# Recurrent-scan attention with a gated unit: order of the result buffers, of the last loads and of the w_o splits

## The chip, the cores and the metric

The kernel runs on one core of a Trainium2 chip. A core has a matrix engine (TensorE, PE in the profile), VectorE (DVE), ScalarE (ACT) and GpSimd (POOL), and a queue engine, SyncE (SP), from which all transfers of this kernel are issued. Each engine works through its own instructions in order and waits at its head for what it needs. The metric is the device time of one execution in microseconds (us); lower is better. Three executions of the kernel before took 2379.27, 2383.05 and 2387.33 us; the median is 2383.05 us.

## The reference

With x of 2048 rows (tokens) and 1024 columns, all float32:

```python
xn = layernorm(x)
q, k, v = split(xn @ wqkv)                     # 32 heads of 32 columns
pq, pk = q @ w_phi, k @ w_phi                  # per head
phi_q = [softmax(pq), softmax(-pq)]            # 64 features a head
phi_k = [softmax(pk), softmax(-pk)]
kv, z = phi_k^T v, sum over tokens of phi_k    # no causal mask
o = (phi_q kv) / (phi_q z + 1e-6)
s = o @ wo                                     # 1024 x 1024
g = silu(((sigmoid(xn @ w_gate)) * (xn @ w_up)) @ w_down)    # inner width 3584
return x + s * g
```

## The kernel before

**Products.** Each float32 operand of a large product is split in two parts, high and low (`split`, line 174): ScalarE rounds it to the high part (line 176), VectorE subtracts to get the low part (line 177). Three matmuls (`mm3`, lines 181 to 183) then stand for one exact product. The products go by a Strassen-like scheme of seven block products instead of eight. Its seven products are called B11, T2, T3, B21, T1, T4 and B22 (line 92); the operands of the T and B22 ones are sums and differences of blocks. A block that shares terms adds onto the bank of an earlier product: B21 onto B11's bank, T4 onto T3's, B22 onto T1's. Before it does, the earlier product must have been read out of the bank.

**Stages.** (1) x is normalised and transposed. (2) For each half of the tokens, V, K and Q are projected, and the gated unit's inner product follows, some 28 units to a half. (3) `w_down` is multiplied in 98 steps (`dsteps`; the list of B22 is gone through once for each half, 14 steps each), and the gate g is written to memory (`g_d`). (4) The last stage works on eight pairs of row tiles (`for tp_ in range(NTP)`). For each pair it computes `o @ wo` in seven products of 12 matmuls, multiplies with the gate, adds x and stores. Between its matmuls it prepares the next pair (`attend`: transposes of the query features, numerators, sums and splits of o).

**w_o.** Its seven operands are made once, during the second half's projections, in four tasks (`o_task`, line 305). A task loads four blocks and splits B11 and B21, splits T4, lets GpSimd make four sums in a row (T1's, T3's, T2's, B22's), and splits these. `keep` splits into one of three buffers (`o_r`) and stores to `wo_d`. `background` lets a task go a step further behind an evacuation (`proj_out`, line 471). During stages 3 and 4 the operands are loaded again (`wo_prep`, line 767) into buffers that have come free: T3's four into block `x1`, which is new at step `ND - 2 * NJ`, and B21's into former buffers of h.

**w_down's loads.** `down_prep` (line 684) loads a weight block into one of two raw buffers (`wdraw`, line 690) and a piece of h into one of three (lines 696 and 700), then splits both. It runs ahead as far as free buffers allow. Side work (`side`) is taken one item for each step after `ND - 2 * NJ`.

**The last stage's buffers.** `res` holds four half buffers, dealt in the same order to every pair: `u1`, `u2`, `y11`, `y21`. `u1` takes B11 (ScalarE's copy, line 1225), then T2 is added (line 1227), and `u2` is `u1` plus T3 (line 1229). The results are: B21 into `y11` (line 1236), T1 into `u2`, T4 into `y21`, B22 into `u1` (line 1239). Each is multiplied with the gate and added to x, on GpSimd in pieces of 256 columns, or on VectorE for T4 and B22 of the last pair (`eng`, line 1233), and stored (line 1242). `gx_load` (lines 1203 and 1204) fetches the gate and x for a result into a ring of four half buffers, two results deep; the next load is asked for when a result has been stored.

**Order.** The program's text gives priorities. A planner (line 1271) lays the instructions of each engine out by its own estimate of durations, so an instruction can stand earlier or later on its engine than its place in the text: in the last pair T1's product stands before B21's. `tc.issue_after(i)` makes instructions follow instruction `i` on that engine.

Of the kernel before, what the change touches and what calls it, by code (L numbers as in the profile page):

```python
# [91 lines left out]
B11, T2, T3, B21, T1, T4, B22 = range(7)  # L92
# [3 lines left out]
def hedgehog_glu_kernel(  # L96
# [12 lines left out]
    nc = tc.nc  # L109
    pool, vector = Pieces(nc.gpsimd, 256), Pieces(nc.vector, 1024)  # L110
# [21 lines left out]
    h_d = dram.tile([7, NJ, P, NCH, HB], F32, name="h_d")  # L132
    wd_d = dram.tile([7, NJ, P, HB], F32, name="wd_d")
# [26 lines left out]
    def whole(i):  # L160
        return slots[i].rearrange("p a n -> p (a n)")

    def halves(*ids):
        return [slots[i][:, a] for i in ids for a in range(2)]
# [24 lines left out]
    side, last_sp = deque(), []  # L189
# [115 lines left out]
    def o_task(k):  # L305

        def keep(i, b):
            o = slots[o_r.next()]
            split((o[:, 0].bitcast(F32R), o[:, 1].bitcast(F32R)), b)
            nc.sync.dma_start(wo_d[i, k], o.bitcast(F32).rearrange("p a n -> p (a n)"))  # L310

        a11, a12, a21, a22 = bs = halves(47, 52)
        for b, (f, h) in zip(bs, ((0, 0), (0, 1), (1, 0), (1, 1))):
            nc.sync.dma_start(b, wo[(k + 4 * h) * P:(k + 4 * h + 1) * P, f * HB:(f + 1) * HB])
        yield
        keep(B11, a11)
        keep(B21, a12)
        yield
        keep(T4, a22)
        pool.add(a22, a21, a22)  # L320
        pool.sub(a21, a11, a21)
        pool.sub(a11, a22, a11)
        pool.sub(a12, a12, a11)
        yield
        yield
        keep(T2, a11)
        keep(T3, a21)
        yield
        keep(T1, a22)
        keep(B22, a12)  # L330

    o_r = Ring((36, 37, 38))
# [316 lines left out]
    wdraw = Ring(halves(42))  # L649
    yr = Ring(halves(48, 49))  # L650
    sig_r = Ring(halves(53))
    last_split = []

    def wd_block(i, j):
        f, col = {B11: (j, 0), B21: (j + NJ, 0), B22: (j + NJ, 1)}.get(i, (j, 1))
        return w_down[f * P:(f + 1) * P, col * HB:(col + 1) * HB]
# [27 lines left out]
    def down_prep():  # L684
        n = len(dready)
        if n == len(dsteps) or not wfree or len(hfree) < len(dsteps[n][2]):
            return False
        i, j, cs = dsteps[n]
        r = wdraw.next()
        nc.sync.dma_start(r, wd_block(i, j) if i in (B11, B21, B22) else wd_d[i, j])  # L690
        w = wfree.popleft()
        split(pair(w), r)
        r = hraw.next()
        hs = {}
        if len(cs) == 2:
            nc.sync.dma_start(whole(r), h_d[i, j].rearrange("p c n -> p (c n)"))
        for c in cs:
            rc = slots[r][:, c]
            if len(cs) == 1:
                nc.sync.dma_start(rc, h_d[i, j, :, c])  # L700
            hs[c] = hfree.popleft()
            last_split[:] = [split(pair(hs[c]), rc).ins]
        dready.append((w, hs))
        return True
# [49 lines left out]
    NTP = TT // 2  # L754
# [2 lines left out]
          T1: [], T4: [], B22: list(range(4))}  # L757
    phu = Ring((44, 20))
    ofr = Ring((46, 24, 25, 26, 27, 22, 23, 39, 40, 41, 42))
    res = Ring(halves(49, 52))  # L760
    gx = Ring(halves(54, 53))
    tpr, nmr, amm = Ring(banks[:2]), Ring(banks[2:4]), Ring(banks[4:])
    e_next, units_ph, of = [0, 0], {}, {}
    oraw = [slots[50], slots[51]]
# [1 line left out]
    def wo_prep(i, k):  # L766
        nc.sync.dma_start(slots[WO[i][k]].bitcast(F32).rearrange("p a n -> p (a n)"), wo_d[i, k])

    def e_load(u):
        tp_, hb = divmod(e_next[u], 2)  # L770
        if tp_ < NTP:
            nc.sync.dma_start(whole(47 + u), f_d[2 * tp_ + u, hb].rearrange("q s n c -> (q s) (n c)"))
        e_next[u] += 1
# [202 lines left out]
    for n, (kind, c, what, i) in enumerate(ops):  # L976
# [37 lines left out]
        j, s = what  # L1014
# [21 lines left out]
        if i == B11:  # L1036
            u1, u2 = ur.next(), ur.next()
# [5 lines left out]
        else:  # L1043
# [3 lines left out]
            g = gates[q]  # L1047
# [46 lines left out]
    u1, u2 = halves(0, 1, 2, 3), halves(4, 5, 6, 7)  # L1094
# [12 lines left out]
    def evacuate(i, p):  # L1107
# [18 lines left out]
        else:  # L1126
            nc.vector.tensor_add(u1[p], u1[p], b)
            gate_out(u1[p], t, 1)

    ND = len(dsteps)  # L1130
    LQ = 64
    late = [Steps(*[(5, lambda t=t, hb=hb: q_task(t, hb)) for hb in range(2) for t in range(a, TT, 2)]) for a in range(2)]
    for n, (i, j, cs) in enumerate(dsteps):
        w, hs = dready[n]
        for c in cs:
            for u in range(4):
                p = 4 * c + u
                mm3(banks[p], cut(pair(hs[c]), slice(u * P, (u + 1) * P)), pair(w),
                    j == 0 and i in (B11, T2, T3, T1), j == NJ - 1, skip_group_check=True)
        wfree.append(w)  # L1140
        hfree.extend(hs.values())
        if n >= ND - 2 * NJ - 8 and len(WO[B21]) < 4 and hfree:
            WO[B21].append(hfree.popleft())
        if n == LQ:
            assert not last_q.left
            block("fb", 43, 4, F32R)
            for q, s in enumerate(KVB):
                nc.sync.dma_start(slots[s].bitcast(F32), kvbd_d[q])
        while down_prep():
            pass  # L1150
        if j == NJ - 1:
            for c in cs:
                for u in range(4):
                    evacuate(i, 4 * c + u)
        if n == 0:
            assert not any(a.left for a in (early_k, proj1, *beside0, *beside1)) and not kv_due
        if n < 2 * NJ * 3 - 2:
            for a in range(2):
                if late[a].left and (n or not a) and late[a].left > 5 * 16 * (80 - n) // 82 - 3 * a:
                    with tc.issue_after(last_split[0]):  # L1160
                        late[a].step()
        if last_q.left and last_q.left > last_q.total * (LQ - n) // (LQ):
            with tc.issue_after(last_split[0]):
                last_q.step()
        if 40 <= n < 56 and n % 2 == 0:
            wo_prep(*divmod((n - 40) // 2, 4))
        if n == ND - 2 * NJ:
            assert not any(a.left for a in late) and len(WO[B21]) == 4
            block("x1", 4, 4, F32R)
            for i in (T3, B21):  # L1170
                side.extend([lambda i=i, k=k: wo_prep(i, k) for k in range(4)])
            side.extend([lambda u=u: e_load(u) for u in range(2)])
        if n == ND - NJ:
            step(1000)
            side.extend([lambda fn=fn, a=a: fn(*a) for fn, *a in attend(0)])
        if len(dready) == ND:
            for i, free in ((T1, hfree), (T4, wfree)):
                while free and len(WO[i]) < 4:
                    WO[i].append(free.popleft())
                    side.append(lambda i=i, k=len(WO[i]) - 1: wo_prep(i, k))  # L1180
        if n > ND - 2 * NJ:
            step(1 + (n > ND - NJ and n % 2))
# [9 lines left out]
    gxs = {}  # L1192
# [5 lines left out]
    def gx_load():  # L1198
        if result:
            tp_, i = result.pop(0)  # L1200
            t, cols = rows(tp_, i)
            g, xt = gxs[tp_, i] = gx.next(), gx.next()
            nc.sync.dma_start(g, g_d[t, :, cols])
            nc.sync.dma_start(xt, x[t * P:(t + 1) * P, cols])

# [3 lines left out]
    for tp_ in range(NTP):  # L1209
        nxt = attend(tp_ + 1) if tp_ + 1 < NTP else []  # L1210
        n = 0
        u1, u2, y11, y21 = [res.next() for _ in range(4)]
        for i in range(7):
            if i in opening:
                abank[i] = amm.next()
            ps = abank[{B21: B11, T4: T3, B22: T1}.get(i, i)]
            o = [h.rearrange("p (k t) -> p k t", t=P) for h in pair(of[tp_][i])]
            for k in range(4):
                mm3(ps, (o[0][:, k], o[1][:, k]), pair(WO[i][k]), i in opening and k == 0, k == 3, skip_group_check=True)
                n += 1  # L1220
                while nxt and (13 - len(nxt)) * 3 <= 2 * n:
                    fn, *a = nxt.pop(0)
                    fn(*a)
            if i == B11:
                nc.scalar.copy(u1, ps)
            elif i == T2:
                nc.vector.tensor_add(u1, u1, ps)
            elif i == T3:
                nc.vector.tensor_add(u2, u1, ps)
            else:  # L1230
                g, xt = gxs.pop((tp_, i))
                t, cols = rows(tp_, i)
                eng = vector if tp_ == NTP - 1 and i in (T4, B22) else pool
                if i == B21:
                    y = y11
                    nc.vector.tensor_mul(y, g, ps)
                else:
                    y = {T1: u2, T4: y21, B22: u1}[i]
                    nc.vector.tensor_add(y, u2 if i == T1 else u1, ps)
                    eng.mul(y, y, g)  # L1240
                eng.add(y, y, xt)
                nc.sync.dma_start(out[t * P:(t + 1) * P, cols], y)
                gx_load()
# [31 lines left out]
```

## Time and profile before

| what | us |
|---|---|
| median of three executions | 2383.05 |
| lowest and highest | 2379.27, 2387.33 |
| the profiled execution's own time | 2388.2 |
| its span, first to last instruction | 2386.4 |
| TensorE busy in the span | 2350.8 |
| TensorE's longest waits after the start | 3.0 (at 2366.8), 2.8 (at 970.7), 2.4 (at 2115.9) |
| last matmul's end | 2379.95 |

The span starts with the first instruction and ends with the last; the profiled execution's own time is 1.8 us longer. In a row of the timeline stand start, duration, engine, line and operation, and in brackets how long the engine had been idle and what released it. "x4" means four instructions merged into one row. A row of waits gives the sum in us, the number and the longest. In rows of DMA issues "to landing" is the time from the issue until the data are in place.

### The profile page before, as it was taken

The page shows a single profiled execution, that of the slowest core. Times are in us where ns is not written, and L with a number is a line of the kernel's source. Part 1 is how long each engine was busy: PE and PEld are TensorE (multiplying, and loading weights), DVE is VectorE, ACT ScalarE, POOL GpSimd, SP SyncE. Part 2 cuts the span into 40 slices and gives each one's busy share as a digit, 9 for nine tenths or more (in the row PEclk, how much of TensorE's full clock was granted, in tenths as well). Part 3 has the DMA queues.
Part 4 walks back from the last instruction along what each step waited for, and adds up shares of the span by engine and source line. Part 5 has one row for each costly group of instructions (what it writes and reads, how often), then busy time and mean ns, then how long its engine had stood idle before and what let it go on. Part 6 is the DMA issues. An engine that isn't in the chain of part 4 may idle for free. (4 is left out here: it accounts for less than half of the span.)

```text
span 2386.4 us, 32555 instructions
## 1 busy us (share of the span) xinstructions
PE 2350.8 (99%) x10772; PEld 1954.1 (82%) x10772; DVE 1654.7 (69%) x2362; ACT 990.4 (42%) x1478; POOL 1180.2 (49%) x1354
## 2 busy tenths in 40 slices
PE   8999999999999999999999999999999999999998
PEld 6788888878888788788888888888888888878886
DVE  7534778677777675466767878765676776567775
ACT  6433344445454453233444334443443333355442
POOL 4510166777777542304463645454444455434665
PEclk9999999999999999999999999999999999999999
DMA  8874566888888789858887888879777777878654
GB/s 293 281 258 172 176 230 216 271 309 296 298 298 295 278 288 332 316 190 294 264 288 280 278 265 263 282 265 354 249 244 247 260 249 240 285 254 284 210 194 151
DMA packets 266426, 626.24 MB, mean 262 GB/s; under 512 B 37904, under 2 KB 66576, under 8 KB 261648
## 3 DMA queue, kind: packets, MB, share of 16 engines
q1 hardware_dynamic: 266256, 624.15, 77.1%
q8 instruction: 85, 1.39, 0.2%
q14 instruction: 85, 0.70, 0.1%
HBM read 374.47 MB, written 249.56 MB: 261 GB/s over the span
## 5 line engine op out<-in xcount | busy, mean ns | idle before, releaser
L182 PE MATMUL bank<-x,w 128*128 128x512 f32 x2352 | 916.7, 390 | 0.0
L181 PE MATMUL bank<-x,w 128*128 128x512 f32 x2352 | 905.1, 390 | 6.7 <-DVE fb L1052 2.4
L183 PE MATMUL bank<-x,w 128*128 128x512 f32 x2352 | 906.2, 390 | 0.0
L79 POOL TENSOR_TENSOR fc<-fc 128x256 f32<-128x256 f32 x486 | 417.5, 889 | 473.1 <-DMA fc<-e_d 114.0
L177 DVE TENSOR_TENSOR w<-fa,w 128x512 fp32r<-128x512 f32 (+1 forms) x444 | 405.1, 915 | 190.4 <-ACT w L176 185.1
L176 ACT CAST w<-fa 128x512 fp32r<-128x512 f32 (+1 forms) x444 | 307.6, 698 | 539.8 <-PE bank L182 339.1
L181 PEld LDWEIGHTS bank<-x,w 128*128 128x128 f32 x2352 | 442.1, 188 | 101.0 <-DVE fb L1052 3.5
L183 PEld LDWEIGHTS bank<-x,w 128*128 128x128 f32 x2352 | 442.0, 188 | 91.7
L182 PEld LDWEIGHTS bank<-x,w 128*128 128x128 f32 x2352 | 442.2, 188 | 90.1
L181 PE MATMUL bank<-w,x 128*128 128x512 f32 x704 | 276.8, 393 | 5.8 <-DVE fb L471 2.8
L182 PE MATMUL bank<-w,x 128*128 128x512 f32 x704 | 275.6, 391 | 1.8 <-DVE w L177 1.8
L183 PE MATMUL bank<-w,x 128*128 128x512 f32 x704 | 275.8, 392 | 0.9 <-DVE x L177 0.9
L79 POOL TENSOR_TENSOR fb<-fa 128x256 f32<-128x256 f32 x112 | 100.5, 918 | 244.5 <-DMA fa<-w_gu 143.8
L79 POOL TENSOR_TENSOR fb<-fb,fc 128x256 f32<-128x256 f32 x132 | 122.5, 948 | 120.5 <-DVE fc L1059 120.2
L181 PEld LDWEIGHTS bank<-w,x 128*128 128x128 f32 x704 | 132.6, 188 | 34.9 <-issue 3.2
L182 PEld LDWEIGHTS bank<-w,x 128*128 128x128 f32 x704 | 132.7, 189 | 29.3 <-DVE w L177 2.6
L183 PEld LDWEIGHTS bank<-w,x 128*128 128x128 f32 x704 | 132.6, 188 | 28.6 <-DVE x L177 1.8
L79 POOL TENSOR_TENSOR fc<-fc,sa 128x256 f32<-128x256 f32 x128 | 97.2, 790 | 94.3 <-issue 85.1
L176 ACT CAST p<-fc 128x512 fp32r<-128x512 f32 x100 | 75.1, 758 | 160.3 <-DVE fc L537 68.2
L177 DVE TENSOR_TENSOR p<-fc,p 128x512 fp32r<-128x512 f32 x100 | 101.3, 1018 | 53.5 <-ACT p L176 53.2
L177 DVE TENSOR_TENSOR x<-fa,x 128x512 fp32r<-128x512 f32 x112 | 91.4, 817 | 45.2 <-ACT x L176 45.1
L176 ACT CAST w<-fb 128x512 fp32r<-128x512 f32 (+1 forms) x114 | 71.2, 626 | 115.2 <-PE bank L182 88.6
(210 smaller groups left out, 2919.3 us busy)
## 6 DMA issues: line engine op xcount, KB each, us to landing
ws_d<-w SPq DMA_DIRECT2D x112, 512.0 KB, 4.1
w<-ws_d SPq DMA_DIRECT2D x112, 512.0 KB, 5.2
fa<-w_gu SPq DMA_DIRECT2D x84, 512.0 KB, 4.6
fa<-h_d SPq DMA_DIRECT2D x84, 512.0 KB, 5.0
fa<-wf_d SPq DMA_DIRECT2D x32, 1024.0 KB, 6.4
h_d<-fc SPq DMA_DIRECT2D x120, 256.0 KB, 4.5
fa<-w_down SPq DMA_DIRECT2D x80, 256.0 KB, 5.2
h_d<-fb SPq DMA_DIRECT2D x76, 256.0 KB, 4.7
```

Source lines behind the costliest of these rows:

```text
L79: last = self.engine.tensor_tensor(o[:, s], a[:, s], b[:, s], op=op)
L176: nc.scalar.copy(o[0], src)
L177: return nc.vector.tensor_sub(o[1], src, o[0].bitcast(F32))
L181: nc.tensor.matmul(o, a[0], b[0], start=first, stop=False, **kw)
L182: nc.tensor.matmul(o, a[0], b[1], start=False, stop=False, **kw)
L183: nc.tensor.matmul(o, a[1], b[0], start=False, stop=last, **kw)
```

## The change

Five edits:

- `o_task` splits T1 and T3 first, then T2 and B22, in two steps as before. Before, T2 and T3 came first, then T1 and B22.
- `last_load` remembers the last load issued by `down_prep`. The loads of w_o for T3 come after those for B21 and the two `e_load` in the side work, and each is put behind the last load so far (`behind_load`).
- `res` is a plain list, and after each pair it is re-dealt: the next pair's `u1` is this pair's `y11`, `u2` stays, `y11` becomes `y21`, and `y21` becomes `u1`.
- Gate and x of the last pair go into eight half buffers of their own (`last_gx`, slots 47, 48, 50 and 51: those of the query features and of the raw operands), and whatever of them is still to be loaded when the last pair starts is loaded at once.
- In the last pair GpSimd multiplies the gates of T4 and B22 with `u1` as soon as T2 is in it and adds the product to x. Afterwards VectorE multiplies T4's and B22's banks with the gate and adds that sum: two passes over 512 columns where there were three.

```diff
@@ o_task @@
+        keep(T1, a22)
+        keep(T3, a21)
+        yield
         keep(T2, a11)
-        keep(T3, a21)
-        yield
-        keep(T1, a22)
         keep(B22, a12)
@@ down_prep @@
-        nc.sync.dma_start(r, wd_block(i, j) if i in (B11, B21, B22) else wd_d[i, j])
+        last_load[:] = [nc.sync.dma_start(r, wd_block(i, j) if i in (B11, B21, B22) else wd_d[i, j]).ins]
...
@@ last stage's buffers @@
-    res = Ring(halves(49, 52))
-    gx = Ring(halves(54, 53))
+    res = halves(49, 52)
+    gx, last_gx = Ring(halves(54, 53)), Ring(halves(47, 48, 50, 51))
...
+    def behind_load(f, *a):
+        with tc.issue_after(last_load[0]):
+            f(*a)
...
             block("x1", 4, 4, F32R)
-            for i in (T3, B21):
-                side.extend([lambda i=i, k=k: wo_prep(i, k) for k in range(4)])
+            side.extend([lambda k=k: wo_prep(B21, k) for k in range(4)])
             side.extend([lambda u=u: e_load(u) for u in range(2)])
+            side.extend([lambda k=k: behind_load(wo_prep, T3, k) for k in range(4)])
...
-            g, xt = gxs[tp_, i] = gx.next(), gx.next()
+            ring = last_gx if tp_ == NTP - 1 else gx
+            g, xt = gxs[tp_, i] = ring.next(), ring.next()
...
-        u1, u2, y11, y21 = [res.next() for _ in range(4)]
+        u1, u2, y11, y21 = res
+        res = [y11, u2, y21, u1]
+        last = tp_ == NTP - 1
+        while last and result:
+            gx_load()
...
             elif i == T2:
                 nc.vector.tensor_add(u1, u1, ps)
+                for r in (T4, B22) if last else ():
+                    (g, xt), t = gxs[tp_, r], gx.next()
+                    pool.mul(t, u1, g)
+                    pool.add(xt, xt, t)
...
-                eng = vector if tp_ == NTP - 1 and i in (T4, B22) else pool
-                if i == B21:
-                    y = y11
+                eng = vector if last and i in (T4, B22) else pool
+                if i == B21 or eng is vector:
+                    y = {B21: y11, T4: y21, B22: u1}[i]
                     nc.vector.tensor_mul(y, g, ps)
```

More of the change, by code (lines that the diff above doesn't have):

```diff
@@ L325, in o_task @@
         yield
-        keep(T2, a11)
+        keep(T1, a22)
         keep(T3, a21)
         yield
-        keep(T1, a22)
+        keep(T2, a11)
         keep(B22, a12)
@@ L651, in hedgehog_glu_kernel @@
     sig_r = Ring(halves(53))
-    last_split = []
+    last_split, last_load = [], []
     def wd_block(i, j):
@@ L695, in down_prep @@
         if len(cs) == 2:
-            nc.sync.dma_start(whole(r), h_d[i, j].rearrange("p c n -> p (c n)"))
+            last_load[:] = [nc.sync.dma_start(whole(r), h_d[i, j].rearrange("p c n -> p (c n)")).ins]
         for c in cs:
@@ L699, in down_prep @@
             if len(cs) == 1:
-                nc.sync.dma_start(rc, h_d[i, j, :, c])
+                last_load[:] = [nc.sync.dma_start(rc, h_d[i, j, :, c]).ins]
             hs[c] = hfree.popleft()
```

## The prediction

> **What bounds the kernel now.** I read the totals first, then what TensorE waited for, then granted clock and matmul counts in short windows, and last the timeline around each wait. The profiled span:
>
> ```profile
> span 2386.4 us, 32555 instructions
> PE 2350.8 (99%) x10772; PEld 1954.1 (82%) x10772; DVE 1654.7 (69%) x2362; ACT 990.4 (42%) x1478; POOL 1180.2 (49%) x1354
> ```
>
> TensorE (PE) is busy all but 35.6 us, and the change alters no matmul. So it can gain only in that 35.6 us, and by a better clock. The list of what PE waited for shows two rows that it aims at (a third, late weights, comes under B):
>
> ```profile
> PE bank L181 <- ACT fc L1225: 4.9, 3, 3.0
> ...
> PE bank L181 <- DVE fb L471: 2.8, 1, 2.8
> ```
>
> L1225 is ScalarE's copy of B11 into `u1`, the first step of a pair of row tiles in the last stage. L471 is an evacuation of a projection product in the second half. Windows of 10 us with PE alone (busy us, count, granted clock, DMA share, GB/s), one undisturbed and then one around each of the three largest stalls:
>
> ```profile
> 960.00:970.00 10.00, 10.00 (x45) 1.00 0.76 292
> 970.00:980.00 10.00, 7.17 (x25) 0.83 0.89 329
> ...
> 2115.00:2125.00 10.00, 7.63 (x27) 0.83 0.60 212
> 2365.00:2375.00 10.00, 6.95 (x24) 0.83 0.37 103
> ```
>
> 45 matmuls fill 10 us, 0.222 us each. The three windows lack 20, 18 and 21, so these stalls cost 4.4, 4.0 and 4.7 us, about 1.6 us more than the gaps of 2.8, 2.4 and 3.05 us themselves. The rows behind the first gap show where the rest goes:
>
> ```profile
> 970.27 0.39 PE L183 MATMUL bank<-w,x 128*128 128x512 f32 x1
> 973.50 0.47 PE L181 MATMUL bank<-w,x 128*128 128x512 f32 x1 [2.83 <-DVE fb L471]
> ...
> 975.06 0.63 PE L181 MATMUL bank<-w,x 128*128 128x512 f32 x1
> ```
>
> A matmul takes 0.63 us instead of 0.39 for some time after the gap: a removed gap of this size is worth 1.6 us more than its length. [...]
>
> **The change part by part.**
>
> **C, result buffers in order of release.** Today `u1` is the same buffer in every pair. It holds the pair's last result, B22, and the next pair's first copy must wait until that is stored.
>
> ```profile
>   DMA out<-fc: 29.5, 7
> ```
>
> That row (of the releasers of L1225) says that ScalarE waited for such a store in seven pairs of eight, 29.5 us in all. Most of it is covered, since PE needs the copy only when B21 adds onto B11's bank; 4.9 us in three pairs isn't. The last pair in detail:
>
> ```profile
> 2362.94 3.27 POOL L79 TENSOR_TENSOR fc<-fc 128x256 f32<-128x256 f32 x4
> 2366.24 0.34 SPq L1242 DMA_DIRECT2D out<-fc  x1
> 2369.24 0.58 ACT L1225 COPY fc<-bank 128x512 f32<-128x512 f32 x1 [7.01 <-DMA out<-fc]
> 2369.88 0.50 PE L181 MATMUL bank<-w,fa 128*128 128x512 f32 x1 [3.05 <-ACT fc L1225]
> ```
>
> After the change `u1` takes the previous pair's B21 buffer. B21's path to its store is one GpSimd (POOL) add, and it starts at least two products before the end of the pair, some 24 matmuls or 5.3 us earlier than B22's, so the copy waits for its own product only. The other three names move to buffers whose stores have five to six products (13 us or more) to land, against a store's 3.1 us (row below). The price is nothing: no instruction is added. I take all of it: 1.85 us (4.9 less 3.05) in two earlier pairs and 4.7 in the last. Bounds: 1.0 if small waits for operands appear there, and no more than 1.85, for the first; 3.0 to 4.7 for the second.
>
> **D, the last pair's tail.** After the last matmul VectorE now does three passes for B22, and T4's last add, ahead of B22's in the queue, waits for a late load of x:
>
> ```profile
> 2379.56 0.39 PE L183 MATMUL bank<-x,fb 128*128 128x512 f32 x1
> 2379.99 0.69 DVE L1239 TENSOR_TENSOR fc<-fc,bank 128x512 f32<-128x512 f32 x1 [0.98 <-PE bank L183]
> 2380.71 0.69 DVE L79 TENSOR_TENSOR fc<-fc 128x512 f32<-128x512 f32 x1
> 2382.00 1.29 DVE L79 TENSOR_TENSOR fc<-fc 128x512 f32<-128x512 f32 x2 [0.60 <-DMA fc<-x]
> ...
> L1242 SPq DMA_DIRECT2D out<-fc x32: 337/338/433, 2195.2 to 2383.3; - x32
> ...
> DMA to landing us min/median/max: 2.0/3.1/6.2
> ```
>
> Afterwards two passes remain: multiply at 2379.99, add at 2380.71 to 2381.40, store issued near 2381.4. The present one goes out at 2383.3 and the span ends 3.1 later; so 1.9 us are saved, if x and the sums made ahead are there. POOL makes them: `u1*g` and `+x` for T4 and B22, four operations in halves, eight instructions, beside the six it has for T1 and B21:
>
> ```profile
> 2375.30 1.43 POOL L79 TENSOR_TENSOR fc<-fc 128x256 f32<-128x256 f32 x2 [0.30 <-DVE fc L1236]
> ```
>
> At 0.72 us each the fourteen take 10.0 us. From 2366.2, where POOL is done with the pair before, that is 2376.2. With the 4.7 us stall gone, the last matmul ends at 2375.25 and VectorE's last pass at 2376.7, so POOL finishes in the same half microsecond. POOL can be later: gates and x for T4 and B22 go into the buffers of the raw operands, whose last split on VectorE ends here:
>
> ```profile
> 2362.27 1.26 DVE L177 TENSOR_TENSOR fa<-fc,fa 128x512 fp32r<-128x512 f32 x1 [2.78 <-ACT fa L176]
> ...
> DMA to landing us min/median/max: 2.7/3.9/6.4
> ```
>
> The four loads (the row is that of the loads of x) issue from 2363.5 at about 0.4 us each and land by 2368 to 2369, so POOL may idle 2 us and the end slip 1.5. Gain 0.4 to 1.9; I take 1.4, since POOL still has T1's and B21's operations for that gap. In SyncE's queue these loads may stand ahead of stores of the pair before and hold them until 2363.5; by the new order of buffers no copy waits for such a store. The same split row shows 1.26 us for a VectorE pass with two SBUF operands beside POOL, against 0.69 alone: 0.6 us that could fall on the last add, within these bounds.
>
> **B, the w_o loads spaced.** Four loads of w_o (T3) wait together for one block and then go out back to back, ahead of weights:
>
> ```profile
> 2107.76 1.79 SPq L767 DMA_DIRECT2D x<-wo_d  x4
> 2109.59 0.97 SPq L690 DMA_DIRECT2D fa<-w_down  x1
> ...
> DMA to landing us min/median/max: 7.9/7.9/8.0
> ...
> DMA to landing us min/median/max: 2.4/3.1/8.0
> ...
> 2109.15 0.62 ACT L176 CAST x<-fa 128x512 fp32r<-128x512 f32 x1 [0.83 <-DVE w L177]
> 2117.57 0.62 ACT L176 CAST x<-fa 128x512 fp32r<-128x512 f32 x1 [6.71 <-DMA fa<-w_down]
> ...
> 2115.48 0.39 PE L183 MATMUL bank<-x,w 128*128 128x512 f32 x1
> 2118.24 2.08 PE L181 MATMUL bank<-x,w 128*128 128x512 f32 x4 [2.37 <-ACT x L176]
> ```
>
> The two w_down loads behind the burst land after 7.9 to 8.0 us; the median of the twelve around them is 3.1. Only two buffers hold raw w_down, so ScalarE's splits stop from 2109.15 to 2117.57, and PE, which had prepared weights until 2115.7, stands until 2118.24. Each T3 load now issues behind the newest load of the product in preparation, one per step of 12 matmuls (2.7 us). A step then moves its own two loads of 256 KB and 512 KB more: 1.05 MB, 390 GB/s for four steps, more than the 329 GB/s window above. At 329 four steps take 12.7 us instead of 10.7, 2 us late, against a reserve of over 5 us (2110.5, the end of the last split, to 2115.7): no stall. At worst every load lands in 8.0 us: two per 9.3 us with the split are 4.65 per step, 1.95 too slow, 7.8 over four steps; less 5.2 of reserve that is a stall of 2.6 plus 1.6 of clock, no better than today (-0.2). Gain -0.2 to 4.0; I take 3.2, nearer to the row at 329. The B21 loads and f_d loads that now stand first are of the same number, into buffers free earlier: no cost.
>
> **A, the w_o splits in order of sums.** In the fourth w_o task the timeline shows:
>
> ```profile
> 963.56 8.04 POOL L79 TENSOR_TENSOR fc<-fc 128x256 f32<-128x256 f32 x8 [18.63 <-DVE p L177]
> 970.27 1.66 ACT L176 CAST p<-fc 128x512 fp32r<-128x512 f32 x3 [5.05 <-POOL fc L79]
> 966.33 1.22 DVE L177 TENSOR_TENSOR w<-fa,w 128x1024 fp32r<-128x1024 f32 x1
> 970.92 1.83 DVE L177 TENSOR_TENSOR p<-fc,p 128x512 fp32r<-128x512 f32 x2 [3.37 <-ACT p L176]
> 972.68 0.67 DVE L471 TENSOR_TENSOR fb<-fc,bank 128x512 f32<-128x512 f32 x1
> ```
>
> POOL makes four sums of two instructions. T2, split first, is the third sum, ready at 970.2. VectorE's half of that split stands in its queue ahead of L471's evacuation; that is late, and PE stands until 973.5. Now T1, the first sum, is split first and T3, the second, next. POOL's three sums take 6.6 us, so the first two are ready near 965.8 and 968.0, and by the two-step chain (0.62 and 0.68) VectorE is done with T3 near 969.6; the evacuation ends at 970.3, just when PE wants it. The split buffers wait for earlier stores:
>
> ```profile
> L310 SPq DMA_DIRECT2D wo_d<-p x3: 319/320/320, 961.6 to 964.1; - x3
> ...
> DMA to landing us min/median/max: 4.1/4.8/4.8
> ```
>
> They land from 966 to 969, no later than the sums need. That would give the whole 4.4. But the order on ScalarE and VectorE is chosen by the program's planner: T2's split may still come ahead of the evacuation, which then starts near 971.5 instead of 972.7, a gain of 1.2. Bounds 0 to 4.4; I take 2.8, the middle of 1.2 and 4.4. No instruction is added, and stores keep their number.
>
> **Sum.** 1.85 + 4.7 + 1.4 + 3.2 + 2.8 = 13.95 us. The profiled execution took 2388.2 us, 1.8 over its span: 2374.2 by its own time. It is 5.1 us above the median of the runs shown (2383.05; 2379.27 to 2387.33), so some of its stalls may be larger than usual. 2383.05 less 13.95 is 2369.1; for that doubt I give up 0.9 us and forecast **2370.0**.
>
> **The rivals.**
>
> 1. All stalls go whole: 1.85 + 4.7 + 1.9 + 4.0 + 4.4 = 16.85, 2366.2. For it: the bare arithmetic of A and B. Against: A's evacuation is in time by tenths only.
> 2. A and B give nothing, since the planner places splits and loads differently from their place in the text: 7.95 from C and D, 2375.1. For it: PE's stalls there hang on in-order queues.
> 3. POOL takes ScalarE's place in the last pair: its fourteen instructions start so late, behind loads, that the pair ends as late as today, and the change doesn't do there what it says. Then 1.85 + 3.2 + 2.8 = 7.85, 2375.2. Against: it needs POOL to be 6 us late where I find 1.5.
> 4. Slower: moved splits block VectorE in the other three w_o tasks. T1's split, wanted earlier, waits at the head of VectorE's queue, and each task gets a stall like that at 970 (4.4). Three new ones cost 13.2 and the old one stays; C, D and B give 11.15: 2385.1. It decides once an evacuation comes over 8 us after its product (three products of 12 matmuls). Against: every split then has its sum no later than now.
>
> **Chances.** Forecast 0.55, first rival 0.14, second 0.18, third 0.06, fourth 0.07. A measurement of this kernel tells about 0.3%, 7.1 us: below 2375.9 is faster, above 2390.2 slower. The forecast lies there but for 0.04, the first rival whole, the second and third at the border, about half: 0.51 + 0.14 + 0.12 = 0.77, rounded down to 0.75 for stalls that a shifted order may make elsewhere. The fourth ends on the slow side of before, mostly within 0.3%; 0.05 is beyond. The range runs from below the first rival to beyond the second and third, 2363 to 2378; the likeliest case's own is 2366 to 2374.
>
> **What would show it.** C: no wait of PE for L1225, and its copies released by PE. D: VectorE's last two passes right after the last matmul, with about 5 us from that to the end instead of 6.45. B: four single wo_d loads between w_down loads, no PE wait for `x L176` there. A: VectorE's splits of `p` waiting less than 3.4 us, and no wait for L471. The forecast is wrong if a new wait of over 2 us on PE appears, or if the end waits for POOL's stores of T1 and B21.

## The result and the profile after

| | before | after |
|---|---|---|
| median of six executions each, us | 2383.56 (2379.27 to 2388.78) | 2369.5 (2367.5 to 2371.29) |
| profiled execution's own time, us | 2388.2 | 2370.45 |
| its span, us | 2386.4 | 2368.7 |
| TensorE busy in the span, us | 2350.8 | 2346.8 |

The ratio is 0.994, with a 95% interval of 0.9927 to 0.9952: 14.1 us faster. The forecast was 2370.0, with a range of 2363 to 2378. The time came out as predicted. Three of its four terms did not: C gave more than its term, A and D less, and that these errors cancel is luck.

The totals of the profile after, then rows of the list of what TensorE (PE) waited for (us in total, times, longest):

```profile
span 2368.7 us, 32568 instructions
PE 2346.8 (99%) x10772; PEld 1953.9 (82%) x10772; DVE 1656.8 (70%) x2360; ACT 992.8 (42%) x1478; POOL 1189.1 (50%) x1362
```

```profile
PE bank L181 <- DVE fb L1052: 3.3, 2, 2.6
...
PE bank L181 <- ACT x L176: 0.6, 1, 0.6
```

No row for the copy of B11 (now line 1234) and none for line 471 is left; what remains for `x L176` is one wait of 0.6 us, at 66 us in the first stage. The same four places in windows with PE alone (busy us, count, granted clock, DMA share, GB/s):

```profile
960.00:970.00 10.00, 10.00 (x46) 1.00 0.83 267
970.00:980.00 10.00, 10.00 (x46) 1.00 1.00 372
2115.00:2125.00 10.00, 10.00 (x46) 1.00 0.52 174
2350.00:2360.00 10.00, 10.00 (x46) 1.00 0.32 107
```

All are full, at a granted clock of 1.00; the last lies in the last pair, where 21 matmuls were missing before. The view of the copy itself says what ended its engine's idle time, and lists nobody after "who waited for it":

```profile
L1234 ACT COPY fc<-bank x8: 578/582/589, 2175.0 to 2347.7; 128x512 f32<-128x512 f32 x8
...
  PE bank L183: 2.6, 2
who waited for it (us, times):
```

No copy waits for a store any more, only for its own product. The loads of w_o in the timeline of SyncE, and of line 690's loads around them the time to landing:

```profile
2102.79 0.32 SPq L767 DMA_DIRECT2D x<-wo_d  x1
2104.20 0.68 SPq L767 DMA_DIRECT2D x<-wo_d  x1
2107.45 0.42 SPq L767 DMA_DIRECT2D x<-wo_d  x1
2110.74 0.42 SPq L767 DMA_DIRECT2D x<-wo_d  x1
```

```profile
DMA to landing us min/median/max: 2.5/3.7/6.0
```

They go out singly, and the slowest w_down load near them lands in 6.0 us where it was 8.0. The fourth w_o task and, below it, the tail of the last pair:

```profile
954.89 6.46 POOL L79 TENSOR_TENSOR fc<-fc 128x256 f32<-128x256 f32 x8 [17.74 <-DVE p L177]
...
964.88 1.29 DVE L177 TENSOR_TENSOR p<-fc,p 128x512 fp32r<-128x512 f32 x2
966.09 0.68 DVE L471 TENSOR_TENSOR fb<-fc,bank 128x512 f32<-128x512 f32 x1
```

```profile
2349.28 14.42 POOL L79 TENSOR_TENSOR fc<-fc 128x256 f32<-128x256 f32 x20
...
2362.16 2.09 DVE L79 TENSOR_TENSOR fc<-fc 128x512 f32<-128x512 f32 x1
2363.61 0.39 PE L183 MATMUL bank<-x,fb 128*128 128x512 f32 x1
2364.17 0.68 DVE L1249 TENSOR_TENSOR fc<-fc,bank 128x512 f32<-128x512 f32 x1
2364.94 0.69 DVE L79 TENSOR_TENSOR fc<-fc 128x512 f32<-128x512 f32 x1
```

After the last matmul two passes remain, as the change says. But T4's last add takes 2.09 us beside GpSimd (POOL), which is at work until 2363.70; so B22's multiply starts at 2364.17, while its product was done at 2364.00.

### The profile page after: what moved, and what is told of

It reads as the page before. It is cut to its first block, busy times and chain, and to the rows that moved or that the text cites. A ratio compares the mean times of both kernels' runs of the same rounds, so it can differ in the third digit from the quotient of the medians.

```text
span 2368.7 us, 32568 instructions
## 1 busy us (share of the span) xinstructions
PE 2346.8 (99%) x10772; PEld 1953.9 (82%) x10772; DVE 1656.8 (70%) x2360; ACT 992.8 (42%) x1478; POOL 1189.1 (50%) x1362
## 5 line engine op out<-in xcount | busy, mean ns | idle before, releaser
L79 POOL TENSOR_TENSOR fc<-fc 128x256 f32<-128x256 f32 x494 | 426.7, 894 | 443.1 <-DMA fc<-e_d 105.9
L176 ACT CAST w<-fa 128x512 fp32r<-128x512 f32 (+1 forms) x444 | 308.2, 698 | 561.7 <-PE bank L182 353.2
L181 PEld LDWEIGHTS bank<-w,x 128*128 128x128 f32 x704 | 132.7, 189 | 30.4 <-ACT w L176 2.1
L176 ACT CAST p<-fc 128x512 fp32r<-128x512 f32 x100 | 75.6, 758 | 135.4 <-DVE fc L537 68.4
L176 ACT CAST w<-fb 128x512 fp32r<-128x512 f32 (+1 forms) x114 | 71.2, 626 | 116.7 <-PE bank L182 91.4
```

The source lines that it names most:

```text
L79: last = self.engine.tensor_tensor(o[:, s], a[:, s], b[:, s], op=op)
L176: nc.scalar.copy(o[0], src)
L181: nc.tensor.matmul(o, a[0], b[0], start=first, stop=False, **kw)
```

## The experiments

Four questions were open: how the 14.1 us divide over the four parts; whether one profiled execution had given the size of each stall; what the tail was worth; and what the 2.6 us wait for line 1052 is. My theory was the prediction's sum. The rivals were that C alone carries it, and that A and B are worth nothing in the time. All kernels compute the whole result.

**Each part undone.** In the kernel after, one part is put back as it was.

C, the buffers dealt in the same order again:

```diff
         u1, u2, y11, y21 = res
-        res = [y11, u2, y21, u1]
```

> The changed kernel with the result buffers dealt in the same order to every pair again (u1 always the last result's buffer). Theory: ScalarE's copy of B11 waits for a store in seven pairs, PE waits for it in two to four of them, 4 to 5 us in all with 3 us in the last pair, the clock falls after that: 2375 to 2377. Rival: in the last pair GpSimd's fourteen instructions set the end by now, so that a late u1 costs only what exceeds them: 2371 to 2373.

B, the loads of T3 ahead of B21's and not put behind another load:

```diff
-            side.extend([lambda k=k: wo_prep(B21, k) for k in range(4)])
+            for i in (T3, B21):
+                side.extend([lambda i=i, k=k: wo_prep(i, k) for k in range(4)])
             side.extend([lambda u=u: e_load(u) for u in range(2)])
-            side.extend([lambda k=k: behind_load(wo_prep, T3, k) for k in range(4)])
```

> The changed kernel with the old order of side work: T3's four w_o loads first, not put behind w_down's loads. Theory: the four go out together near 2100 us, the w_down loads behind them land after about 8 us instead of 3 to 6, PE waits 2 to 2.5 us for weights (x, L176), and the time is about 4 us above 2369.5: 2373 to 2374.5. Rival: the stall was an accident of one execution's transfers: the four loads go out together and PE doesn't wait, 2369 to 2370.

A, the splits in the old order:

```diff
-        keep(T1, a22)
+        keep(T2, a11)
         keep(T3, a21)
         yield
-        keep(T2, a11)
+        keep(T1, a22)
         keep(B22, a12)
```

> The changed kernel with the old order of the w_o splits (T2 and T3 first, then T1 and B22). Theory: each edit removes its own stall. Then PE waits 2 to 3 us for L471 near 970 us again, the granted clock falls there, and the time is 4.4 us above the changed kernel's 2369.5: 2373 to 2375. Rival: the planner's rearrangement as a whole moved the work, and this edit alone does nothing: no wait of over 1 us for L471, 2369 to 2370.

D, neither buffers of their own, nor loads at once, nor sums ahead:

```diff
-            ring = last_gx if tp_ == NTP - 1 else gx
+            ring = gx
...
-        while last and result:
-            gx_load()
...
-                for r in (T4, B22) if last else ():
-                    (g, xt), t = gxs[tp_, r], gx.next()
-                    pool.mul(t, u1, g)
-                    pool.add(xt, xt, t)
...
-                if i == B21 or eng is vector:
-                    y = {B21: y11, T4: y21, B22: u1}[i]
+                if i == B21:
+                    y = y11
```

> The changed kernel without the last pair's own buffers for gate and x, without loading them at once and without the sums made ahead (VectorE's three passes for T4 and B22 again); the new order of result buffers stays. Theory: the end comes 6.2 to 6.5 us after the last matmul instead of 4.7, no other wait changes, 2371 to 2372. Rival: GpSimd's extra eight instructions cost in the last pair what the sums save (VectorE's add of T4 took 2.09 us beside them): 2369 to 2370.

Then, to see what holds again, the kernel after and two of these once more, and C by itself in the kernel before:

```diff
-    res = Ring(halves(49, 52))
+    res = halves(49, 52)
...
-        u1, u2, y11, y21 = [res.next() for _ in range(4)]
+        u1, u2, y11, y21 = res
+        res = [y11, u2, y21, u1]
```

> The changed kernel again, beside the two that undo one edit. Theory: 2368 to 2371, with no wait of PE for L471, for x L176 near 2100 us, or for the copy of B11; the only wait of over 2 us is that of L1052 near 785 us, where the program is the same as before. Rival: some execution of it stalls there too: over 2372.

> The changed kernel with T3's four w_o loads issued together as before, once more: the first time its median lay 3.6 us above the changed kernel's, while its profiled execution showed only 0.45 us of waiting at the burst. Theory: the wait at the burst differs between executions (0.4 to 2.4 us, with the slower clock behind the long ones) and this is most of the difference: 2371 to 2374, and this profile shows another length of the wait. Rival: the 3.6 us came from the wait near 785 us, which both kernels have: 2368 to 2371 this time.

> The changed kernel with the old order of the w_o splits, once more: the first time its median lay 0.9 us above the changed kernel's, from 2366.6 to 2374.5, and its profiled execution had no wait for L471. Theory: the stall near 970 is there in some executions only, those over 2373; the median is 0 to 2 us above the changed kernel's beside it. Rival: it was a lucky profile, the stall is the rule: 3 us and more above.

> The kernel before with nothing changed but the order in which the four result buffers are dealt. Theory: undoing it cost 9.5 us, so alone it brings 6.5 to 9.5: 2373.5 to 2376.5; no wait of PE for L1225, and the end comes 5 to 5.5 us after the last matmul instead of 6.45, since loads and stores of the last pair are no longer late. Rival: alone it brings what the profile before showed, 4.9 us of waits and 1.6 of clock: 2376.5 to 2377.5, the other 3 us needing the other edits.

Measured (medians; the ratio is to the kernel before on the same chip; the difference is to the kernel after). The kernel after ran beside the last four, where it took 2369.52 us; the first undoing of each part, on another chip and without it, is compared with the 2369.5 us of the result:

| kernel | us | ratio, 95% | against after |
|---|---|---|---|
| after, again | 2369.52 | 0.994 (0.9928 to 0.9953) | |
| without C | 2378.97 | 0.9985 (0.9975 to 0.9994) | +9.5 |
| without B | 2373.07 | 0.9962 (0.9949 to 0.9974) | +3.6 |
| without B, again | 2371.6 | 0.9948 (0.9935 to 0.996) | +2.1 |
| without A | 2370.36 | 0.9948 (0.9935 to 0.9962) | +0.9 |
| without A, again | 2369.46 | 0.9938 (0.9923 to 0.9953) | -0.1 |
| without D | 2369.03 | 0.9947 (0.9933 to 0.996) | -0.5 |
| C alone, in the kernel before | 2371.39 | 0.995 (0.9936 to 0.9963) | +1.9 |

Several expectations missed. Without C the time was above the expected 2375 to 2377 us, C alone was below 2373.5 to 2376.5; without A and without D it fell short of 2373 to 2375 and of 2371 to 2372, and came out near the 2369 to 2370 of their rivals. Without B the time was as expected, but not the wait of 2 to 2.5 us.

**C.** It is the bulk by both routes: 9.5 us when taken out, and 12.7 when put in alone (2384.12 less 2371.39). The two agree within the second's interval, which is 8.8 to 15.3 us. A cleaner measure is inside one execution, from the last matmul of stage 3 to the last of the kernel, and from there to the end of the span. The two rows that bound it, before, after, with C alone, and without C:

```profile
2177.41 0.39 PE L183 MATMUL bank<-x,w 128*128 128x512 f32 x1
```

```profile
2169.81 0.39 PE L183 MATMUL bank<-x,w 128*128 128x512 f32 x1
```

```profile
2169.84 0.39 PE L183 MATMUL bank<-x,w 128*128 128x512 f32 x1
...
2363.16 0.39 PE L183 MATMUL bank<-x,fb 128*128 128x512 f32 x1
```

```profile
2168.73 0.39 PE L183 MATMUL bank<-x,w 128*128 128x512 f32 x1
...
2373.07 0.39 PE L183 MATMUL bank<-x,fb 128*128 128x512 f32 x1
```

| kernel | last stage, start to start of matmuls, us | from there to the end, us |
|---|---|---|
| before, in three profiles | 202.15, 203.32, 201.67 | 6.86, 7.11, 6.48 |
| without C | 204.34 | 5.62 |
| C alone | 193.32 | 5.61 |
| without D | 193.32 | 5.73 |
| after, in two profiles | 193.80, 193.32 | 5.06, 5.05 |

With C in it the stage takes 193.3 to 193.8 us, whatever else is undone; without it, over 200. From the first profile before to the first after the gain is 8.35 us and not the 6.55 of the sum. In the kernel without C the waits and their cause are back (the list of waits, the releasers of the copy, and its last row on ScalarE):

```profile
PE bank L181 <- ACT fc L1233: 5.3, 4, 2.3
```

```profile
  DMA out<-fc: 25.0, 6
  POOL fc L79: 5.3, 1
```

```profile
2362.75 0.58 ACT L1233 COPY fc<-bank 128x512 f32<-128x512 f32 x1 [6.12 <-DMA out<-fc]
```

So what the copy waits for is the store of `u1`, as the prediction had it. D's loads and sums do not help it.

Where the extra 1.8 us come from was counted in the profile before: a matmul of 512 columns normally starts 0.2265 us after the one ahead of it, and what its starts lie further apart in the last stage adds up to 8.84 us (after: 0.48). Of this 5.35 is at the three waits for the copy, where the rows of waits give 4.9. The rows count from the modelled end of a matmul, 0.39 us after its start, so each is about 0.16 short. 0.98 is at two small waits that the prediction left out:

```profile
2298.97 0.39 PE L182 MATMUL bank<-x,fb 128*128 128x256 f32 x1 [0.39 <-DVE x L177]
```

They are gone in all ten profiles with C in them, where ScalarE is not held at a copy. For the one shown the path is seen: VectorE stood until the late copy, at 2293.06, and then worked with no pause of over 0.3 us up to the split that TensorE waits for. For the other, at 2232.93, it was not traced. Of the last 2.5, 1.6 are matmuls at a granted clock of 0.50 in the last pair, as the sum had it (1.65). The other 0.9 lie at full clock, most of it in the second matmul behind a wait, which starts 0.33 us after the first instead of 0.23.

**B.** Undone, the burst is there again (timeline of SyncE, landing of the two w_down loads behind it, and PE):

```profile
2104.20 1.87 SPq L767 DMA_DIRECT2D x<-wo_d  x4
```

```profile
DMA to landing us min/median/max: 7.6/7.7/7.9
```

```profile
2114.44 1.20 PE L181 MATMUL bank<-x,w 128*128 128x512 f32 x4 [0.45 <-ACT x L176]
```

The late landing comes with the burst: in the profile before and in the first without B the two loads behind it land after 7.6 to 8.0 us, while from 2100 to 2135 us no w_down load takes more than 6.0 us in the profile after and in the first ones without A, C and D, where the loads are spaced. How long TensorE waits varies: 2.4, 1.5 and 2.2 us in three profiles of the kernel before, 0.9 with C alone, 0.45 and 1.8 without B; 0 in all eight with the loads spaced. The second of those without B, in a window of 20 us around it with PE alone:

```profile
2105.00:2125.00 20.00, 18.22 (x74) 0.91 0.67 225
```

74 matmuls where a full window of 20 us counts 90 (the window under A): 16 fewer, 3.6 us. In the first profile without B the place lost only 0.7 us, though the median is 3.6 us up; the wait for line 1052 was longer there (3.2 us against 2.6 in the profile after), and that wait is in both kernels. Without B the five executions lay between 2372.29 and 2376.71 us, clear of those of the result (2367.5 to 2371.29); the second time they lay between 2369.88 and 2373.36, among those of the kernel after beside them (2368.44 to 2373.41). So the burst and its loss are shown in the traces, and the size in the time only roughly.

**A.** Undoing it cost 0.9 and -0.1 us, nothing that these runs can tell, and neither profile shows a wait at line 471. In the first of them VectorE was as late behind a split as the prediction said, and TensorE had no gap there (VectorE and GpSimd in the timeline, the window with PE alone):

```profile
957.57 8.08 POOL L79 TENSOR_TENSOR fc<-fc 128x256 f32<-128x256 f32 x8 [17.47 <-DVE p L177]
964.94 1.86 DVE L177 TENSOR_TENSOR p<-fc,p 128x512 fp32r<-128x512 f32 x2 [3.36 <-ACT p L176]
966.72 0.67 DVE L471 TENSOR_TENSOR fb<-fc,bank 128x512 f32<-128x512 f32 x1
```

```profile
960.00:980.00 20.00, 20.00 (x90) 1.00 0.89 309
```

The chain is the same; it merely stood some 6 us earlier. That raised the question of how usual the 2.8 us of the profile before were.

**The kernel before, profiled twice more.** No edit.

> The kernel before, one more profile of it. Theory: the late copy of u1 is in every execution, and its waits vary; the stall near 970 (L471) isn't in most. So no wait of over 1 us for L471, and 5 to 9 us of waits for L1225 in three to five pairs. Rival: the first profile is the rule: 2.8 us for L471, 4.9 for L1225.

> As before_2, a third profile of the kernel before: it tells how often each of the three stalls (L471 near 970, x L176 near 2115, L1225 in the last stage) occurs. Theory: L1225 in all three profiles, L471 in one, x L176 in all with different lengths. Rival: all three stalls in all profiles.

The first took 2384.66 us, the second 2385.81. Rows of their waits:

```profile
PE bank L181 <- ACT fc L1225: 5.8, 4, 2.7
...
PE bank L181 <- DVE fb L471: 0.6, 1, 0.6
```

```profile
PE bank L181 <- ACT fc L1225: 5.1, 3, 2.4
...
PE bank L181 <- DVE fb L471: 1.3, 1, 1.3
```

The waits for the copy are stable (4.9, 5.8, 5.1); the one at line 471 is 2.8, 0.6 and 1.3, in all three and not in one as my theory had it. Up to that place six profiles ran the same instructions with the old order of splits. To compare them, the start of GpSimd's eight sums is moved by the matmuls that each execution was ahead or behind at 950 us (0.2265 us for each):

| kernel, old order of splits | sums start, us | matmuls by 950 us | start, moved | wait at line 471, us |
|---|---|---|---|---|
| before | 963.56 | 4275 | 963.6 | 2.8 |
| before, third profile | 964.56 | 4263 | 961.8 | 1.3 |
| before, second profile | 962.63 | 4268 | 961.0 | 0.6 |
| C alone | 960.99 | 4274 | 960.8 | 0.2 |
| without A | 957.57 | 4279 | 958.5 | 0 |
| without A, again | 960.40 | 4263 | 957.7 | 0 |

The later the sums start against the matmuls, the longer TensorE waits, nearly one for one beyond 960.6. The profile on which the prediction rested was the latest of the six. With the new order the same reckoning gives 952.8 to 952.9 in seven profiles and 955.6 in the eighth: the sums start 2 to 11 us sooner. They wait for blocks of w_o, whose loads stand in SyncE's queue behind stores of earlier splits: from 905 to 975 us these stores wait 30.4 us for VectorE's splits in the profile before, 18.3 in the one after, and the fourth task's loads issue from 945.9 to 953.2 us before and from 935.8 to 944.1 after. So A does move the task away from the stall.

What the place cost, by starts of matmuls as above, is 4.9, 0.9 and 1.5 us in the three profiles before, 0.4 with C alone, and 0 in all others, those without A among them. So A can have been worth 1 to 5 us in the kernel before while undoing it in the kernel after costs nothing; A alone in the kernel before was not run. What makes the start with the old order drift by 6 us over the same instructions, and why both kernels without A are the earliest, stays open.

**D.** The time without it is 0.5 us lower, which is within the spread. The last column of the table of the last stage does show it: 5.73 us without D, 5.05 and 5.06 with it, so 0.7 and not 1.4. C alone has already taken 1.25 of the 6.86 us, because the late load of x, which the prediction gave to D, goes with C as well. In the profile before, SyncE issued it only at 2377.36 us, behind gate loads and a store that were themselves late:

```profile
2376.88 0.43 SPq L1242 DMA_DIRECT2D out<-fc  x1
2377.36 0.42 SPq L1204 DMA_DIRECT2D fc<-x  x1
```

D alone removes it too: without C, B22's passes also stand right behind the last matmul (5.62 us). VectorE's last passes with C alone, and without D:

```profile
2363.58 0.69 DVE L1240 TENSOR_TENSOR fc<-fc,bank 128x512 f32<-128x512 f32 x1 [0.53 <-PE bank L183]
2364.30 1.42 DVE L79 TENSOR_TENSOR fc<-fc 128x512 f32<-128x512 f32 x2
```

```profile
2361.45 0.69 DVE L1246 TENSOR_TENSOR fc<-fc,bank 128x512 f32<-128x512 f32 x1 [0.52 <-PE bank L183]
2362.17 0.69 DVE L79 TENSOR_TENSOR fc<-fc 128x512 f32<-128x512 f32 x1
2363.02 0.69 DVE L79 TENSOR_TENSOR fc<-fc 128x512 f32<-128x512 f32 x1 [0.16 <-DMA fc<-x]
```

Three passes right behind the matmul, 2.1 to 2.3 us; with D two passes of 1.46 us, which start 0.2 late.

**Past the change.** Two faults were left in the kernel after: the 2.6 us wait for line 1052, and the slow add in the tail. VectorE's row ahead of that wait, and the wait:

```profile
779.93 0.69 DVE L507 TENSOR_REDUCE stq<-p 128x16 f32<-128x512 f32 x1 [4.54 <-DMA r_d<-stq]
782.75 0.50 PE L181 MATMUL bank<-x,w 128*128 128x512 f32 x1 [2.57 <-DVE fb L1052]
```

A reduction stands at the head of VectorE's queue until `stq`, a single tile of sums, has been stored by the tile before; the evacuation at line 1052 stands behind it. The first kernel gives the stored part a tile of its own. The second also lets VectorE do T1's two passes in the last pair, to have GpSimd finish sooner:

```diff
+        if query:
+            r2 = small.tile([P, 32], F32, name=f"rq{name}", tag="rq", bufs=1)
```

> The changed kernel with a buffer of its own for the reciprocals that q_features stores (before, the next tile's first reduction had to wait on VectorE until that store had landed). Theory: the wait of PE for L1052 near 785 us, 2.4 to 5.3 us in the profiles of the changed kernel with a slower clock behind it, comes from there; it shrinks below 1 us, and the time falls by 2.5 to 5: 2364.5 to 2367. Rival: VectorE is simply full there, the evacuation is late without that store too: 2368.5 to 2370.

```diff
-                eng = vector if last and i in (T4, B22) else pool
-                if i == B21 or eng is vector:
+                eng = vector if last and i in (T1, T4, B22) else pool
+                if i == B21 or last and i in (T4, B22):
```

> As w_stats, and in the last pair T1 is multiplied and added on VectorE too, which leaves GpSimd four instructions fewer. Theory: GpSimd's instructions beside it made VectorE's add of T4 take 2.09 us instead of 0.69, and so B22's multiply was 0.1 to 0.2 us late; now that add takes 0.7 us, the end comes 4.4 to 4.6 us after the last matmul instead of 4.7, a gain too small for the times. Rival: the add stays slow, since it is a queue or a port that holds it, and not GpSimd's work: 2 us again.

They took 2365.71 us (2365.2 to 2367.62; ratio 0.9927, 0.9914 to 0.994) and 2365.41 us (2364.28 to 2369.68; 0.9926, 0.9912 to 0.994). The kernel before took 2383.44 us in their round. So the first kernel is 17.7 us below it where the kernel after is 14.6 below in its own round (2384.12 and 2369.52): the tile is worth 3 to 4 us (3.8 by the medians, 3.1 by the two rounds), and all but the slowest of its six executions lie below every one of the kernel after. The window around the place, all engines, in the kernel after and with the tile (busy us and count of PE, PEld, DVE, ACT, POOL, then clock, DMA share, GB/s):

```profile
760.00:820.00 60.00, 57.43 (x246) 46.76 (x245) 42.14 (x57) 24.36 (x36) 47.70 (x58) 0.97 0.82 289
```

```profile
760.00:820.00 60.00, 60.00 (x266) 49.71 (x265) 45.73 (x62) 28.25 (x40) 46.02 (x52) 1.00 0.85 299
```

20 matmuls more in 60 us are 4.5 us. The second edit is worth nothing that can be measured. In the tail T4's add is back at its usual time, but T1's two passes take the same kind of loss earlier:

```profile
2355.51 2.88 DVE L79 TENSOR_TENSOR fc<-fc 128x512 f32<-128x512 f32 x2
...
2359.08 0.69 DVE L79 TENSOR_TENSOR fc<-fc 128x512 f32<-128x512 f32 x1
```

From the end of the last matmul to the end of the span it is 4.55 us, against 4.66 with the tile alone.

## Why the prediction was right, and where it was not

The total came within 0.5 us of the median. The mechanisms of C and B held, and the kernel's gain is mostly theirs; that the total fits this closely is luck, since C was 3 us above its term and A and D together some 3 us below. The sum was 13.95; with the stage and the tail for C and D, and the times of undoing for B and A, the terms were 9.6 (C), 0.6 (D), 2.1 to 3.6 (B) and -0.1 to 0.9 (A), together 12.2 to 14.7.

- **C: right mechanism, too small.** The step "1.85 us (4.9 less 3.05) in two earlier pairs and 4.7 in the last" made 6.55; the last stage's matmuls gained 8.35. The clock's part of it was right. The step took the waits at their rows' length, which is 0.16 short for each (0.45 in all), counted no wait but those for line 1225 (0.98 at two others went with them), and left out the slower start behind each wait (most of 0.9). The tail's 1.2 us came on top. "The price is nothing" held: no wait of the last stage in the profile after names a store.
- **D: "I take 1.4" was mis-sized.** The tail did shorten by 1.8 us, from 6.86 to 5.06, but not by D alone. It was long for two reasons, and the step gave both to D. The late load goes with C as well; beside C, 0.6 to 0.7 us remain for the passes. The warning that the 0.6 us loss beside GpSimd "could fall on the last add" was the right fear with too small a size: T4's add took 1.4 us longer. The forecast that POOL finishes near the last VectorE pass also missed, on the safe side: it was done at 2363.70, ahead of the last matmul's end, and the end did not wait for its stores.
- **B: right.** The value was 3.2; undoing it cost 3.6 and 2.1 in the time, and 0.7 and 3.6 at the place itself. The lower bound's case, in which every load lands in 8.0 us, did not come: none near the place took more than 6.0.
- **A: mis-sized.** "I take 2.8, the middle of 1.2 and 4.4" treats the stall of one profile as what the kernel always pays. The chain of steps was found as described, but its length was the longest of six: the place cost 4.9 us in that profile, 0.9 and 1.5 in the two others of the kernel before. Undoing A gave the lower bound, 0. The new order also did more than the step says: it moved the whole task forward, its sums starting 2 to 11 us sooner, where the step only exchanged splits within the task.
- **The clock.** That a gap costs more than its length held: filled gaps left a clock of 1.00 in all four windows. In the last pair alone 1.6 us went with the slow matmuls. A window also counts the matmuls that its edges cut, so the prediction's 0.222 us for each should be 0.2265; by starts its three stalls cost 4.9, 4.2 and 4.9 us, not 4.4, 4.0 and 4.7.
- **What would make it wrong.** "A new wait of over 2 us on PE": the 2.6 us for line 1052 is not new. The same instructions run there before and after, and the twelve profiles of them show 1.7 to 5.3 us of idle TensorE in the stretch from 770 to 800 us.
- **The rivals.** All stalls going whole (2366.2) is 3.3 us below the median, as A and D gave less than it needs. That A and B give nothing fell on B, by the traces and by one of two comparisons of the time; undoing A cost nothing that shows, as this rival has it, though the stall at its place is in all three profiles before. POOL in ScalarE's place fell: the window 2350 to 2360 has 46 matmuls. The slower rival fell: no evacuation in the other w_o tasks holds TensorE up.

## What to carry to other kernels

When output buffers are dealt in turn, deal them by when each is stored, so that the first one wanted is the first one free; it costs no instruction and was worth two thirds of this change or more. Take the size of a stall from several profiles of the same program, since a wait that hangs on a race between two engines varied here from 0 to 2.8 us. And when one stall is removed, ask which smaller waits and which late loads behind it in the same queues go with it, before giving them to another edit.

## What the runs showed of the hardware

- **The clock fell after some gaps of 1.8 to 2.6 us and not after others of that length.** In the stretch from 770 to 800 us TensorE was idle once in each of twelve profiles. With 2.4 to 2.6 us of idle time, in five profiles, the granted clock over the 30 us was 1.00 in two of them and 0.94 in three; with 1.8 us it was 1.00 in one and 0.94 in another. With 1.7 us (two profiles) and 2.0 us (one) it was 1.00, with 3.2 and 5.3 us (one each) 0.89. In the profile before it also fell to 0.50 behind the gaps of 2.83, 2.37 and 3.05 us. In the first stage, where short gaps follow one another, it fell at 15.97 us in the profile after, where no gap so far was over 1.62 us, and at 22.47 us in the profile before, inside a gap of 2.15 us. In these two profiles each stretch at 0.50 that ended before the last matmul lasted 3.41 us, but for the one in the first stage of the profile after, which lasted 10.24 us. What decides between gaps of like length was not shown.
- **A VectorE add of two SBUF operands took 2.09 us beside GpSimd, where it takes 0.69.** In the profile after, GpSimd's pieces beside it took their usual 0.74 to 0.75 us (median 0.74), so VectorE alone lost time there: 1.40 us, about two of GpSimd's pieces. With the tile of its own the add took 2.08 us; with the second edit too, where GpSimd was done at 2357.11 us, it started at 2359.08 and took 0.69. The loss isn't always VectorE's, nor always as large. Without C the same add took 0.80 us, though GpSimd was at work until 2374.34 us. And at 2350.02 us in the profile after, beside a VectorE split of 1.25 us, one of GpSimd's pieces took 1.19 us. VectorE's passes that read a bank kept to 0.69 us beside the same GpSimd work (at 2358.60 and 2361.38 us). What decides which of the two engines loses was not shown.
